# Two key copies trade engines, V7 moves by half a group, L0 passes a mask, and a memset moves two slots

## The chip, the cores and the metric

The kernel runs on one core of one Trainium2 chip. The metric is device time in microseconds. Before the change it was 331.88 us, the median of 3 runs (331.34 to 332.10). The profiled execution took 331.49 us, of which the profile spans 329.6 us, with TensorE granted its full clock throughout.

## The reference

Batched sparse attention is followed by a bilinear feed-forward network (FFN). Batch 8, 8 heads, 576 positions, 64 dimensions; half the heads see a local window of 32 positions, the other half see every 32nd position.

```python
scores = scale * np.matmul(q, k.transpose(0, 1, 3, 2))
mask_local = (rel >= 0) & (rel < stride)
mask_strided = (rel >= 0) & (pos[None, :] % stride == pos[:, None] % stride)
...
attn = attn / (np.sum(attn, axis=-1, keepdims=True) + 1e-09)
attn_out = np.matmul(attn, v)
...
x = attn_out.transpose(0, 2, 1, 3).reshape(B * S, H * D)     # 4608 x 512
out = (x @ w_a) * (x @ w_b) @ w_out                          # 512 -> 1536 -> 512
```

## The kernel before

The FFN runs over nine tiles of 512 tokens (t = 0 to 8). Each tile is sixteen slots: twelve of `ffn_ab`, which each make one 128-wide block of x @ w_a and x @ w_b on TensorE, copy the first product to SBUF on ScalarE (a_sb, L592) and multiply it with the second on VectorE (pf, L597), and four slots of output matmuls (`ffn_y`, L762, for tiles 0 and 1; `ffn_ys`, a form with fewer products, for tiles 2 to 8). Slot numbers run on, so slot 16 is the first of tile 1.

Attention is woven into these slots. The attention of batch 0 comes first, by the list `ORDER`. For each later batch a table places short steps at slot positions: `STEPS` for batches 1 and 2, `LATER` for the rest. A whole number means after that slot; a number ending in .5 means in the middle of the following slot (between the two FFN matmul groups, or after six of the twelve output matmuls). Batch 1 is spread over slots 5 to 15 of tile 0. The order of every engine is the order in which the program emits instructions; no scheduler changes it, so an instruction that waits holds up all that follow on its engine.

The steps have these names, where c is a pair of heads (0 and 1 local, 2 and 3 strided) and u is half of a pair (u = 2c or 2c + 1):

- Tk and Tq transpose keys and queries of pair c on TensorE into the PSUM tile tp, and copy them to SBUF in `T_e`: keys to kT1l (local) or kT1s (strided) at L306, queries at L314. For batch 1, line 306 puts the keys of c = 0 and c = 2 on ScalarE and those of c = 1 and c = 3 on VectorE.
- Pk and Pq (`pair_up`, L275) first bring two local heads side by side with a copy on VectorE, so that one transpose does both.
- S makes scores in the PSUM tile st (L383), exponentiates them on ScalarE into p (L391) and masks p with a bitwise AND on VectorE (L401).
- V multiplies p by the values into the PSUM tile o (L437), then takes a reciprocal (L445) and multiplies by it (L460), both on VectorE.
- X transposes the attention output into xT, which the FFN of tile 1 reads.
- L (`lead_vl`, L230) copies the leading 32 rows of each block of local values from the end of the block ahead of it, on VectorE. The second and later matmuls of V0 read what L0 writes.
- W (`fast_w`, L174) sums pairs of output weights on VectorE, for the tiles 2 to 8.

From slot 2 on there is one buffer of tp, one of o and one of st, and three buffers of mm for the FFN products. So the transposes of one step wait until the copy of the step ahead of it has emptied tp, and a V step waits until the multiply of the V step ahead of it has read o.

The table `at` places other work after a slot. `zero_qz` (L121) clears query buffers of two batches with memsets on VectorE; the four entries of buffer 0 (read from batch 2 on) come after slots 0, 2, 3 and 5. `spread_vs` (L246), also on VectorE, follows slots 6 to 9.

Of the kernel before, what the change touches and what calls it, by code (L numbers as in the profile page):

```python
# [16 lines left out]
RS = 8  # L17
NP = 72
GP = 80
# [3 lines left out]
PAD = 32  # L23
# [7 lines left out]
def kernel(  # L31
# [10 lines left out]
    nc = tc.nc  # L42
# [135 lines left out]
    def blocks(nm, z):  # L178
        z = int(z)
        return sb.tile([128, 2, (S, RS * GP)[z]], BF16, tag=f"t{nm}{z}", name=f"t{nm}{z}", bufs=1)  # L180
# [117 lines left out]
    def T_e(b, c, nm):  # L298
        tv = held.pop((b, c, nm))
        if c < 2:  # L300
            perm = lambda t: t.rearrange("d (p r) -> d p r", r=RL)
        else:
            perm = lambda t: t.rearrange("d (g p) -> d g p", p=GP)[:, :, :NP]
        if nm == "k":
            t = kT_buf[b % 2][c // 2][:, c % 2]
            (nc.scalar.copy if (b, c) in ((1, 0), (1, 2)) else nc.vector.tensor_copy)(perm(t[:, PAD:] if c < 2 else t[:, :RS * GP]), tv)  # L306
        elif b == 0:
            if c % 2 == 0:
                tl[b, c // 2, nm] = blocks("q", c // 2)
            nc.scalar.copy(perm(tl[b, c // 2, nm][:, c % 2]), tv)  # L310
        else:
            for j in range(2):
                pr = slice(64 * j, 64 * j + 64)
                (nc.vector.tensor_copy if (c, j) == (3, 1) else nc.scalar.copy)(  # L314
                    perm(qz_buf[b % 2][j][c // 2][pr, c % 2]), tv[pr])
# [38 lines left out]
    def step_Tk(b, c):  # L354
        T_p(b, c, "k")
        T_e(b, c, "k")

    def step_Tq(b, c):
        T_p(b, c, "q")
        T_e(b, c, "q")  # L360
# [159 lines left out]
    def step_X(b, c):  # L520
        X_p(b, c)
        X_e(b, c)

    PART = {"Tkp": lambda c: T_p(0, c, "k"), "Tke": lambda c: T_e(0, c, "k"), "Tqp": lambda c: T_p(0, c, "q"),
            "Tqe": lambda c: T_e(0, c, "q"), "Sp": lambda u: S_p(0, u), "Sx": lambda u: S_x(0, u),
            "Sm": lambda u: S_m(0, u), "Vp": lambda u: V_p(0, u), "Vr": lambda u: V_r(0, u), "Vn": lambda u: V_n(0, u),
# [7 lines left out]


    STEPS = {1: {5.5: "Tk2", 6: "Tk3", 6.5: "Tq2", 7.5: "S4 Tq3", 8: "S5", 8.5: "V4", 9: "S6 Pk0", 9.5: "V5 Pq0",
                 10: "Tk0 S7", 10.5: "V6 Tq0 Pk1", 11: "V7 Pq1", 11.5: "Tk1 S0 W0 W1", 12: "Tq1 W2", 12.5: "S1 X2 L0",
                 12.75: "V0 S2 W3", 13: "L1 V1 X3 W4", 13.5: "S3 X0", 14: "V2", 14.5: "V3", 15: "X1"},
             2: {20: "S0", 20.5: "S1", 21.5: "V0", 22: "S2", 23: "V1", 23.5: "S3", 24.5: "V2", 25: "S4", 26: "V3", 26.5: "S5",
                 27.5: "V4", 28: "S6", 28.5: "V5", 29: "S7", 29.5: "V6", 30.5: "V7"}}  # L540
# [246 lines left out]
    with tc.manual_schedule(engines={ENG.PE, ENG.SP, ENG.Pool, ENG.DVE, ENG.Activation}):  # L787
# [29 lines left out]
        for nm in ORDER:  # L817
            if nm[0] == "*":
                spin(int(nm[1:]))
            elif nm == "C0":  # L820
                for x, cp, n in ((raw[0], nc.vector.tensor_copy, "k"), (raw[1], nc.scalar.copy, "q")):
                    t = nats[0, n, False][:, 0:2].rearrange("p h r d -> p (h r d)")
# [42 lines left out]
        def do(i, fn, *args):  # L865
            at.setdefault(i, []).append(lambda: fn(*args))
# [29 lines left out]
            do(6 + h, spread_vs, 1, h, nc.vector.tensor_copy)  # L896
        do(1, zero_qz, 1, nc.vector, ((1, 1),))
        do(4, zero_qz, 1, nc.vector, ((1, 0),))
        for i, jz in ((2, (0, 0)), (3, (1, 0)), (0, (0, 1)), (5, (1, 1))):
            do(i, zero_qz, 0, nc.vector, (jz,))  # L900
        do(14, rezero, 1)
        do(27, fill_v, vl_buf[1])
# [53 lines left out]
```

## Time and profile before

| stretch, us | length | TensorE busy | VectorE busy | ScalarE busy | GpSimd busy |
|---|---|---|---|---|---|
| 28 to 36 | 8.00 | 7.81 | 3.94 | 3.72 | 7.74 |
| 36 to 44 | 8.00 | 7.89 | 7.83 | 5.72 | 3.40 |
| 44 to 52 | 8.00 | 6.48 | 5.90 | 4.36 | 4.15 |
| 52 to 62 | 10.00 | 9.89 | 7.51 | 5.42 | 6.84 |

Each row is a stretch of the span in which steps of batch 1 run; a busy time is the sum of the instructions' recorded time in it. A TensorE that is busy for nearly the whole stretch may still wait a little, because records overlap and a few are missing. What counts for the end is where TensorE stands still, and which engine's instruction it stands still for. The second row shows VectorE with hardly any free time, the first shows it half idle.

The change touches these instructions, with the times at which they start in the profiled execution:

| instruction | engine | start, us | duration, ns |
|---|---|---|---|
| memset qz01s (L121) | VectorE | 30.94 | 592 |
| key copy of Tk2, kT1s (L306) | ScalarE | 31.22 | 638 |
| V7's matmuls (L437) | TensorE | 44.46 | 8 matmuls, 0.42 us in all |
| key copy of Tk1, kT1l (L306) | VectorE | 47.04 | 746 |
| L0's copy, vl (L230) | VectorE | 51.02 | 422 |

### The profile page before, as it was taken

The numbers are of one execution on the slowest core, as the hardware profiler recorded it, in microseconds if no ns is written. First come the engines' busy times: TensorE is split into PE (matmuls) and PEld (weight loads), VectorE is DVE, ScalarE is ACT, GpSimd is POOL, SyncE is SP. The second block draws the span as 40 slices with busy tenths as digits, with TensorE's granted clock in tenths as the row PEclk, the third lists the DMA queues.
The fourth block names the chain that finished last, engine by engine and source line by source line (L and its number), as shares of the span: only waits on it lengthen the run. The fifth ranks groups of instructions, "written<-read, shape, count | busy, mean of one in ns | idle before, by whom it ended". The sixth has DMA issues, their size and how long they took to land.

```text
span 329.6 us, 7647 instructions
## 1 busy us (share of the span) xinstructions
PE 321.1 (97%) x2793; PEld 206.3 (63%) x2824; DVE 265.6 (81%) x509; ACT 201.1 (61%) x325; POOL 176.3 (53%) x294
## 2 busy tenths in 40 slices
PE   8999988999999999999999999999999999999995
PEld 6764555455555577556999995559555954584474
DVE  6757796889867999999999999999878944657662
ACT  5763756358778766887577756776787543313321
POOL 8946636897867655775577556855302131232021
PEclk9999999999999999999999999999999999999999
DMA  9999999599999699899998988998024022004004
GB/s 152 155 203 195 204 183 172 144 164 147 112 213 115 110 80 86 85 172 158 90 76 140 198 84 72 138 211 90 20 58 132 2 67 64 0 2 127 0 3 127
DMA packets 98837, 37.50 MB, mean 114 GB/s; under 512 B 76656, under 2 KB 95984, under 8 KB 98800
## 3 DMA queue, kind: packets, MB, share of 16 engines
q0 software_dynamic: 85936, 19.48, 66.0%
q1 hardware_dynamic: 12576, 17.34, 18.3%
q8 instruction: 22, 0.36, 0.5%
q10 hardware_dynamic: 288, 0.20, 0.2%
q14 instruction: 15, 0.12, 0.2%
HBM read 39.51 MB, written 9.44 MB: 149 GB/s over the span
## 4 chain that ended last, share of the span: by engine, by line
PE 83%; DMA 11%; POOL 4%; issue 1%; DVE 0%; POOLq 0%; ACT 0%; DVEq 0%
PE mm L575 50%; PE mm L680 17%; PE mm L762 5%; DMA wb_sb<-in_moe_w_b_dram 4%; DMA vl<-in_v_dram 4%; PE st L383 4%; PE o L481 4%; DMA shared<-in_q_dram 2%; PE mm L708 2%; DMA ql<-in_q_dram 1%; POOL wa_sb L251 1%; POOL wo_sb L254 1%; PE end L708 1%; POOL vs L109 1%; POOL wb_sb L251 0%
## 5 line engine op out<-in xcount | busy, mean ns | idle before, releaser
L575 PE MATMUL mm<-xT,wa_sb 128*128 128x512 bf16 (+1 forms) x453 | 108.9, 357 | 0.9
L575 PE MATMUL mm<-xT,wb_sb 128*128 128x512 bf16 (+1 forms) x466 | 109.4, 357 | 0.3
L592 ACT COPY a_sb<-mm 128x512 f32<-128x512 f32 x106 | 62.0, 585 | 47.6 <-PE mm L575 46.5
L922 POOL CAST pace<-pf 1x1 f32<-1x1 bf16 x84 | 31.3, 373 | 83.0 <-DVE pf L595 80.7
L575 PEld LDWEIGHTS <-wb_sb 128*128 128x128 bf16 x480 | 46.2, 98 | 43.9
L595 DVE TENSOR_TENSOR pf<-a_sb,mm 128x512 bf16<-128x512 f32 x84 | 56.4, 671 | 17.0 <-PE mm L575 13.8
L575 PEld LDWEIGHTS <-wa_sb 128*128 128x128 bf16 x480 | 42.7, 98 | 31.8 <-issue 0.2
L391 ACT ACTIVATE p<-st 128x576 bf16<-128x576 f32 (+1 forms) x64 | 41.5, 649 | 14.1 <-PE st L383 13.4
L490 ACT ACTIVATE xr<-o 64x576 f32<-64x576 f32 x48 | 31.1, 647 | 25.1 <-PE o L481 24.8
L680 PEld LDWEIGHTS <-ps 128*128 128x128 bf16 x360 | 34.5, 98 | 3.9
L491 ACT ACTIVATE xr<-xr 64x576 f32<-64x576 f32 x48 | 32.8, 683 | 1.5
L495 DVE TENSOR_TENSOR xT<-o,xr 64x288 bf16<-64x288 f32 x48 | 21.5, 447 | 7.6 <-ACT xr L491 7.1
L497 DVE TENSOR_TENSOR xT<-o,xr 64x288 bf16<-64x288 f32 x48 | 21.5, 448 | 6.4 <-ACT xr L491 5.3
L680 PE MATMUL mm<-wf,ps 128*128 128x256 bf16 x216 | 26.4, 273 | 0.0
L401 DVE TENSOR_TENSOR p<-p,mask_l 128x576 int16<-128x576 int16 x32 | 22.3, 696 | 2.4 <-ACT p L391 2.4
L762 PE MATMUL mm<-wo_sb,pf 128*128 128x512 bf16 x91 | 22.8, 379 | 0.2
L242 POOL DMA_DIRECT2D vs<-in_v_dram x24 | 19.6, 818 | 3.4 <-PE st L383 2.2
L211 POOL DMA_DIRECT2D kl<-in_k_dram x24 | 16.3, 678 | 7.4 <-issue 3.9
L597 DVE TENSOR_TENSOR pf<-a_sb,mm 128x512 bf16<-128x512 f32 x22 | 14.8, 672 | 5.8 <-ACT a_sb L592 4.9
L922 POOL COPY pace<-y_sb 1x1 f32<-1x1 f32 x16 | 2.8, 175 | 30.5 <-ACT y_sb L663 14.6
L211 POOL DMA_DIRECT2D ql<-in_q_dram x24 | 16.0, 666 | 5.2 <-DMA wo_sb<-in_moe_w_out_dram 4.1
L680 PE MATMUL mm<-wf,pf 128*128 128x256 bf16 x144 | 17.6, 273 | 0.0
(162 smaller groups left out, 503.1 us busy)
## 6 DMA issues: line engine op xcount, KB each, us to landing
out_dram<-y_sb SPq DMA_DIRECT2D x12, 512.0 KB, 4.8
out_dram<-y_sb SPq DMA_DIRECT2D x10, 256.0 KB, 3.2
vl<-in_v_dram POOLq DMA_DIRECT2D x6, 384.0 KB, 6.8
kl<-in_k_dram POOLq DMA_DIRECT2D x24, 72.0 KB, 3.1
ql<-in_q_dram POOLq DMA_DIRECT2D x24, 72.0 KB, 3.2
vs<-in_v_dram POOLq DMA_DIRECT2D x24, 72.0 KB, 3.7
wo_sb<-in_moe_w_out_dram POOLq DMA_DIRECT2D x4, 384.0 KB, 11.5
natk<-in_k_dram POOLq DMA_DIRECT2D x20, 72.0 KB, 3.5
```

Of the source, the lines that this page charges most:

```text
L211: nc.gpsimd.dma_start(out=t[32 * h:32 * h + 32], in_=src[b, h].rearrange("(i y) d -> y i d", y=32))
L391: nc.scalar.activation(p[:M, :, :W], st[:M, :, :W], ACT.Exp, scale=scale)
L401: nc.vector.tensor_tensor(pi, pi, mk, op=ALU.bitwise_and)
L490: nc.scalar.activation(r, sums, ACT.Ln)
L491: nc.scalar.activation(r, r, ACT.Exp, scale=-1.0)
L495: nc.vector.tensor_mul(dst[:, W * half:W * (half + 1)], o[:64, j, :W], r[:, j])
L575: nc.tensor.matmul(ps_[:, c0:c0 + n], lhsT=w[:, kk, 128 * f:128 * (f + 1)], rhs=xT[:, kk, x0:x0 + n], start=(kk == first and c0 == 0), sto ...
L592: nc.scalar.copy(a_sb, ab[0])
L595: nc.vector.tensor_mul(pf[:, f, :].rearrange("p (i a s) -> p a i s", i=2, s=16), halves(a_sb), halves(ab[1]))
L680: nc.tensor.matmul(bank[b][:, q], lhsT=lhs(g, q), rhs=rhs(g), start=new and q == 0 and g == 0, stop=g == FG - 1, skip_group_check=True)
L762: nc.tensor.matmul(ybank[j], lhsT=pf[:, f, 128 * j:128 * (j + 1)], rhs=wo_sb[:, f], start=(f == 0), stop=(f == FD - 1))
L922: nc.gpsimd.tensor_copy(pace, done)
```

## The change

Four edits of order and engine; nothing computed changes. The keys of batch 1 that go to ScalarE are now those of both local pairs (c = 0, 1) and not those of c = 0 and 2: Tk2's copy goes to VectorE and Tk1's to ScalarE. This is meant to leave ScalarE free for the FFN copies around slot 6 and VectorE free around slot 12. V7 moves from the end of slot 11 to the middle of slot 12, behind S0, so that TensorE need not wait there for the output tile o. L0 goes ahead of S1, so that VectorE does its copy before the mask of S1, which waits for ScalarE. And the memset of the strided half of query buffer (0, 1) moves from slot 5 to slot 7, which clears the place for Tk2's copy.

```diff
@@ T_e @@
-            (nc.scalar.copy if (b, c) in ((1, 0), (1, 2)) else nc.vector.tensor_copy)(perm(t[:, PAD:] if c < 2 else t[:, :RS * GP]), tv)
+            (nc.scalar.copy if b == 1 and c < 2 else nc.vector.tensor_copy)(perm(t[:, PAD:] if c < 2 else t[:, :RS * GP]), tv)
@@ STEPS @@
-                 10: "Tk0 S7", 10.5: "V6 Tq0 Pk1", 11: "V7 Pq1", 11.5: "Tk1 S0 W0 W1", 12: "Tq1 W2", 12.5: "S1 X2 L0",
+                 10: "Tk0 S7", 10.5: "V6 Tq0 Pk1", 11: "Pq1", 11.5: "Tk1 S0 V7 W0 W1", 12: "Tq1 W2", 12.5: "L0 S1 X2",
@@ zero_qz @@
-        for i, jz in ((2, (0, 0)), (3, (1, 0)), (0, (0, 1)), (5, (1, 1))):
+        for i, jz in ((2, (0, 0)), (3, (1, 0)), (0, (0, 1)), (7, (1, 1))):
             do(i, zero_qz, 0, nc.vector, (jz,))
```

## The prediction, made before the changed kernel was run

> **What bounds the kernel now.** I read the shares first, then TensorE's waits, then the timelines of the four engines around each wait.
>
> ```profile
> PE 321.1 (97%) x2793; PEld 206.3 (63%) x2824; DVE 265.6 (81%) x509; ACT 201.1 (61%) x325; POOL 176.3 (53%) x294
> ```
>
> TensorE (PE) has work nearly all the time, so only what moves its queue can move the end. Asked who TensorE waited for, the trace names three waits in the stretch that the diff touches (columns: total us, times, longest) and none from 62 us to the end:
>
> ```profile
> PE o L437 <- DVE vl L230: 0.7, 1, 0.7
> PE tp L286 <- DVE kT1l L306: 0.5, 1, 0.5
> PE o L437 <- DVE xr L460: 0.2, 1, 0.2
> ```
>
> Busy time by stretch agrees: TensorE has its holes between 44 and 52 us (6.48 of 8 us).
>
> ```profile
> 36.00:44.00 8.00, 7.89 (x91) 1.00 1.30 202
> 44.00:52.00 8.00, 6.48 (x72) 1.00 1.98 161
> ```
>
> The timeline (start, duration) shows the last hole's cause: VectorE (DVE) held the copy of leading rows behind a mask, and the mask behind ScalarE's exp.
>
> ```profile
> 49.84 0.65 ACT L391 ACTIVATE p<-st 128x576 bf16<-128x576 f32 x1 [0.28 <-PE st L383]
> ...
> 50.53 0.46 DVE L401 TENSOR_TENSOR p<-p,mask_l 128x576 int16<-128x576 int16 x1 [0.97 <-ACT p L391]
> ...
> 51.02 0.42 DVE L230 COPY vl<-vl 32x704 bf16<-32x704 bf16 x1
> 51.49 0.31 PE L437 MATMUL o<-vl,p 128*128 128x65 bf16 x5 [0.75 <-DVE vl L230]
> ```
>
> Two more holes are put down to nobody. The sixth FFN matmul group starts at 32.40, when ScalarE's copy ends (32.35), and the transposes of Tq2 start at 33.49, when VectorE's key copy ends (33.43):
>
> ```profile
> 31.22 0.64 ACT L306 COPY kT1s<-tp 128x576 bf16<-128x576 bf16 x1 [1.40 <-PE tp L295]
> 31.76 0.59 ACT L592 COPY a_sb<-mm 128x512 f32<-128x512 f32 x1
> ...
> 32.38 0.69 DVE L597 TENSOR_TENSOR pf<-a_sb,mm 128x512 bf16<-128x512 f32 x1 [0.85 <-ACT a_sb L592]
> ...
> 32.98 0.45 DVE L306 COPY kT1s<-tp 128x576 bf16<-128x576 bf16 x1
> ...
> 33.49 0.42 PE L295 MATMUL tp<-ident,shared 72*128 72x72 bf16 x8
> ```
>
> All holes together are some 1.9 us (0.2 + 0.2 + 0.22 + 0.50 + 0.75): a ceiling for the gain.
>
> [...] the trace has 638 ns for both ScalarE key copies, 451 ns for the strided keys and 746 ns for the local keys on VectorE. [...] the copy vs (L246) takes 279 ns alone and 451 ns at 40.90, beside a GpSimd DMA issue (40.53 to 41.26). I use that 0.17 us as what one collision costs.
>
> **The change, part by part.** Every operation and shape occurs in the trace of before, so only the waits are new.
>
> 1. *Tk2's key copy from ScalarE to VectorE.* ScalarE loses 638 ns at 31.22; VectorE gains 451 ns there, in the place of the memset (592 ns, 30.94) that leaves; it is otherwise idle to 32.38. The FFN copy a_sb can start when its matmuls end (30.9) and no longer holds the next group, so the hole at 32.40 goes. The product pf then waits for the other matmul group, ending at 32.05; one group earlier that wait ended 0.11 after the matmuls, so it starts at 32.16, not 32.38. The next key copy ends at 33.21 and Tq2 starts at 33.27: TensorE is **0.22 us ahead**.
>
> 2. *The memset of qz01s, 592 ns, two slots later.* It lands behind the copy vs at 36.48, in front of the mask of S4. From 35.88 to 44.67 VectorE shows no idle time at all: everything queued behind it (masks, normalisations, pair copies, pf) moves. Consecutive VectorE instructions overlap by 0.08, so it adds 0.51; part 1 brings the head of this queue 0.22 forward, so VectorE is 0.29 late. TensorE's weight load for V5 waits for the normalisation of V4, which ended at 39.75 and now at 40.04: load at 40.09, against 40.01. Tk0's load waits for the pair copy that ended at 40.98, now 41.27: load at 41.31, against 41.12. TensorE is now **0.19 us late**, having lost 0.41. V6 and Tq0 have 0.3 us of slack (42.19 to 42.49, 42.60 to 42.93) and wait no longer than that.
>
> 3. *V7 half a group later.* TensorE would be free at 44.24 + 0.19 = 44.43. It no longer waits for xr (0.22 gone) but does six output matmuls first (1.30). Tk1 starts at 45.73, against 46.01; S0 and V7 follow, and V7's work (0.25) is put back there. On VectorE V7's reciprocal and multiply (0.20 + 0.69) now stand behind the mask of S0.
>
> 4. *Tk1's key copy from VectorE to ScalarE.* ScalarE has ended a_sb by 45.5. The copy runs from 46.19 to 46.83 (638 ns), so Tq1, which TensorE reaches at about 47.15, does not wait: the 0.50 hole goes. The exp of S0 now queues behind it: 46.85 to 47.50, 0.12 later than before.
>
> 5. *L0 ahead of S1's mask.* L0's own input, the load of vl, has landed at 47.24. VectorE now does: mask of S0 47.55 to 48.00, V7 to 48.80, three wf (1.48 together) to 50.28, L0 50.20 to 50.62. V0's second matmul goes at 50.67 instead of 51.49. TensorE reaches V0 near 49.9, so it still waits some 0.75 there: the wait stays, but on a chain that starts earlier. The mask of S1 moves behind L0, to 51.0; V1 needs it at 52.2. It is free.
>
> Sum at V0: **0.82 us ahead**. Behind it every step hangs on TensorE's progress (reciprocals after V0, then S2, X3, L1), and after 62 us TensorE waited for nobody, so I carry the lead to the end: 331.88 - 0.82 = 331.06, rounded to 331.1.
>
> **The rivals.**
>
> A, *the memset is absorbed*: VectorE regains its 0.29 before V5 and Tk0, TensorE keeps its 0.22 and the whole chain to V0 moves 0.41 more: 331.06 - 0.41 = 330.65. [...] Against: no idle in 35.88 to 44.67.
>
> B, *the memset passes in full*: the head of the VectorE queue does not move (0.51 late, plus one collision of 0.17, so 0.68). Tk0's load is at 41.7, TensorE is 0.58 late instead of 0.19, and V0 goes at 51.06: 331.06 + 0.39 = 331.45. For it: TensorE hangs on VectorE at 40.0 and 41.1 with 0.1 us to spare. Against: GpSimd's issues are few there.
>
> C, *the new chain to V0 becomes the bound*, so it is slower: mask, reciprocal, multiply, three wf and L0 now stand in line from S0's exp. If each of these seven is hit by a collision (7 x 0.17 = 1.2) on top of B's 0.39, V0 goes at 52.26, 0.77 later than before: 331.88 + 0.77 = 332.65. For it: GpSimd issues DMAs at 47.52, 49.52 and from 50.17. Against: wf kept 546 ns beside those issues before.
>
> A fourth possibility gives no change: the lead is lost later, where VectorE is 97% busy (110 to 130 us), leaving 331.9. TensorE shows no wait on VectorE there, and VectorE's work moves along with it.
>
> **How the numbers follow.** Forecast 0.50, A 0.13, B or the later loss 0.25, C 0.12. The bar of 0.2% is 0.66 us, and the forecast clears it by 0.16 only, so of its 0.50 I count 0.42 as faster and 0.08 as same. B and the later loss give same 0.22 and slower 0.03. Faster 0.55, same 0.30, slower 0.15. The range goes from a little under A, 330.4, to the later loss with some scatter of the runs (331.34 to 332.10), 332.0; C is left out.
>
> **What would show it.** Step 1: Tq2's transposes start near 33.3. Step 2: the memset lies near 36.5, and Tk0's transposes start later than 41.33, near 41.5. Step 3: no wait for xr near 44.2. Step 4: no wait of tp for kT1l. Step 5: a wait of V0 for vl of 0.6 to 0.9 us ending near 50.7. The prediction is wrong if Tk1 starts later than 46.0, if V0's wait ends after 51.2, or if TensorE shows waits after 62 us that before did not have.

## The result, and the profile after

The changed kernel took 330.38 us (median of 6 runs, 329.97 to 330.96), against 331.61 us for the kernel before in the same series: a ratio of 0.9964, 95% interval 0.9949 to 0.9979. Measured once more on another occasion it gave 330.74 us against 331.58 us, ratio 0.9976 (0.9966 to 0.9987). So the change saves 0.8 to 1.2 us, and both intervals lie below 1. The forecast was 0.8.

TensorE's waits over the whole span of the changed kernel (total us, times, longest us); the first stands at the kernel's start and was there before too:

```profile
PE misc L153 <- PEq L940: 0.9, 1, 0.9
PE mm L762 <- DMA wo_sb<-in_moe_w_out_dram: 0.7, 1, 0.7
```

All three waits of before are gone, V0's wait for L0 too, and one has come that the prediction did not name: output matmuls (L762) wait for a load of wo_sb, the output weights. TensorE's busy time in the two stretches shown before (length, busy, granted clock, DMA share, GB/s):

```profile
36.00:44.00 8.00, 7.95 (x88) 1.00 1.32 202
44.00:52.00 8.00, 7.34 (x87) 1.00 1.81 151
```

The stretch with the holes went from 6.48 to 7.34 us busy. What remains is mostly the new wait, seen in the timeline (start, duration) of four engines:

```profile
45.46 0.64 ACT L306 COPY kT1l<-tp 128x576 bf16<-128x576 bf16 x1 [0.53 <-PE tp L286]
...
45.99 0.66 ACT L391 ACTIVATE p<-st 128x576 bf16<-128x576 f32 x1
46.58 0.81 PE L762 MATMUL mm<-wo_sb,pf 128*128 128x512 bf16 x3 [0.66 <-DMA wo_sb<-in_moe_w_out_dram]
...
47.90 1.48 DVE L174 TENSOR_TENSOR wf<-wo_sb 128x768 bf16<-128x768 bf16 x3
...
49.41 0.35 DVE L230 COPY vl<-vl 32x704 bf16<-32x704 bf16 x1
...
49.94 0.34 PE L437 MATMUL o<-vl,p 128*128 128x65 bf16 x6
```

The key copy and the exp lie one behind the other on ScalarE, as step 4 has it. TensorE then stands still for the third of the four pieces of wo_sb. VectorE does not stand still meanwhile: it runs through its line to L0, which ends at 49.76, and V0's six matmuls go in one piece at 49.94.

**How the runs are compared.** The profiled spans differ by 1.5 us (329.6 and 328.1), but not all of that is the change: Tk2's first transpose, ahead of which TensorE has the same instructions in every kernel, starts at 30.76 and 30.26 us, and over all profiles here between 30.23 and 31.15. From the first FFN matmul of tile 1 to the end it is 269.4 to 269.5 us in every profile in which that matmul is recorded. So I read each profile from Tk2's first transpose to tile 1's first matmul: 29.35 us before, 28.33 after. Where that last record is missing I take V3's first matmul plus 1.89 us, the distance in all the others. The stretch falls into five parts, by the first matmul of each step:

| kernel | Tk2 to Tq2 | Tq2 to Tk0 | Tk0 to Tk1 | Tk1 to Tq1 | Tq1 to tile 1 | sum | ratio to before, 95% interval |
|---|---|---|---|---|---|---|---|
| before | 2.73 | 7.84 | 4.68 | 1.83 | 12.27 | 29.35 | |
| changed | 2.52 | 8.17 | 4.05 | 2.22 | 11.37 | 28.33 | 0.9964 (0.9949 to 0.9979) |
| after_again | 2.52 | 8.30 | 4.05 | 1.41 | 12.04 | 28.32 | 0.9976 (0.9966 to 0.9987) |
| l0_alone | 2.74 | 7.84 | 4.57 | 1.94 | 11.37 | 28.46 | 0.9978 (0.9971 to 0.9985) |
| v7_alone | 2.74 | 7.83 | 4.04 | 1.64 | 12.20 | 28.45 | 0.9972 (0.9961 to 0.9983) |
| keys_alone | 2.52 | 8.17 | 4.66 | 1.62 | 12.20 | 29.17 | 0.9987 (0.9979 to 0.9995) |
| memset6 | 2.51 | 7.84 | 4.04 | 1.41 | 12.02 | 27.82 | 0.9944 (0.9930 to 0.9958) |
| memset5 | 2.51 | 7.84 | 4.04 | 1.41 | 12.02 | 27.82 | 0.9958 (0.9944 to 0.9971) |
| no_l0 | 2.51 | 8.16 | 4.05 | 1.41 | 12.39 | 28.52 | 0.9979 (0.9970 to 0.9988) |
| no_v7 | 2.52 | 8.41 | 4.65 | 1.21 | 11.39 | 28.18 | 0.9959 (0.9947 to 0.9971) |
| no_keys | 2.74 | 7.83 | 4.05 | 1.63 | 11.61 | 27.86 | 0.9964 (0.9952 to 0.9976) |
| no_wo_wait | 2.51 | 8.33 | 4.05 | 1.41 | 12.18 | 28.48 | 0.9974 (0.9967 to 0.9981) |
| w_late | 2.51 | 7.84 | 4.04 | 2.37 | 11.37 | 28.13 | 0.9938 (0.9924 to 0.9952) |
| best | 2.51 | 7.84 | 4.04 | 1.41 | 11.37 | 27.17 | 0.9939 (0.9927 to 0.9951) |

Most parts repeat to 0.01 or 0.02 us where the same wait ends them, so one profile tells more of an edit than the times do, whose intervals are 0.5 to 1.0 us wide. The part from Tq2 to Tk0 is an exception where the memset stands in it: 8.16 to 8.41.

### The profile page after: what moved, and what is told of

It reads as the page before. It is cut to its first block, busy times and chain, and to the rows that moved or that the text cites. A ratio compares the mean times of both kernels' runs of the same rounds, so it can differ in the third digit from the quotient of the medians.

```text
span 328.1 us, 7680 instructions
## 1 busy us (share of the span) xinstructions
PE 322.6 (98%) x2824; PEld 206.5 (63%) x2824; DVE 265.7 (81%) x509; ACT 201.2 (61%) x325; POOL 176.7 (54%) x294
## 4 chain that ended last, share of the span: by engine, by line
PE 84%; DMA 9%; POOL 5%; issue 1%; POOLq 0%; ACT 0%; DVE 0%; DVEq 0%
PE mm L575 51%; PE mm L680 17%; PE mm L762 6%; DMA shared<-in_q_dram 5%; PE st L383 4%; DMA wo_sb<-in_moe_w_out_dram 4%; PE o L481 4%; POOL shared L196 2%; PE mm L708 2%; POOL wa_sb L251 1%; POOL vl L224 1%; PE end L708 1%; POOL wb_sb L251 0%; POOL tk L237 0%; PE tp L506 0%
## 5 line engine op out<-in xcount | busy, mean ns | idle before, releaser
L575 PE MATMUL mm<-xT,wa_sb 128*128 128x512 bf16 (+1 forms) x472 | 110.3, 357 | 0.0
L762 PE MATMUL mm<-wo_sb,pf 128*128 128x512 bf16 x96 | 23.4, 379 | 0.7 <-DMA wo_sb<-in_moe_w_out_dram 0.7
```

The costliest lines, as they stand in the source:

```text
L575: nc.tensor.matmul(ps_[:, c0:c0 + n], lhsT=w[:, kk, 128 * f:128 * (f + 1)], rhs=xT[:, kk, x0:x0 + n], start=(kk == first and c0 == 0), sto ...
L762: nc.tensor.matmul(ybank[j], lhsT=pf[:, f, 128 * j:128 * (j + 1)], rhs=wo_sb[:, f], start=(f == 0), stop=(f == FD - 1))
```

## The experiments

### Each edit alone

**L0 ahead of S1, alone (l0_alone).**

```diff
-12.5: "S1 X2 L0"
+12.5: "L0 S1 X2"
```

> The kernel before with the leading-row copy L0 ahead of S1 as the only edit. 'The stretch' is the time from the first FFN matmul of slot 6 to the first FFN matmul of tile 1: 30.22 us in the profile of before (29.89 to 60.11), 29.38 in that of after (29.21 to 58.59). Theory, each edit's gain depends on which wait ends last: VectorE is free after the three weight sums (49.55 before), L0 runs there to 49.9, and V0, which TensorE reaches at 50.55, doesn't wait: the stretch is 0.75 shorter, 29.5, the time 0.7 us lower. Rival, the load of vl sets L0: L0 is no earlier than before and nothing changes.

The part from Tq1 to tile 1 went from 12.27 to 11.37, and V0 no longer waits; the ratio of 0.9978 is 0.7 us. L0 was free to start at 49.4 and the load of vl did not hold it. The theory stands. (I read from Tk2, not from slot 6's first matmul, because Tk2's transposes waited 0.3 for a load here.)

**V7 half a group later, alone (v7_alone).**

```diff
-11: "V7 Pq1", 11.5: "Tk1 S0 W0 W1"
+11: "Pq1", 11.5: "Tk1 S0 V7 W0 W1"
```

> The kernel before with V7 in the middle of slot 12 as the only edit. Theory: TensorE starts the output matmuls 0.38 earlier (44.08), Tk1's key copy on VectorE no longer stands behind V7's normalisation and ends near 47.0, so Tq1 starts some 0.8 earlier, and S1, its mask and L0 follow: V0's wait stays but ends near 50.6: the stretch is some 0.9 shorter, 29.3. Rival, V7's normalisation now stands in the chain to L0 and takes the gain back: the stretch is 0.0 to 0.3 shorter.

Tk0 to Tk1 fell by 0.64 (0.25 of it V7's own matmuls, which come after Tk1 now) and Tk1 to Tq1 by 0.19 although V7 is now within it. The sum is 0.90 shorter, the time 0.93 us (331.41 x 0.0028). V0's wait stays, as the theory has it:

```profile
PE o L437 <- DVE vl L230: 0.7, 1, 0.7
```

**The keys and the memset, alone (keys_alone).**

```diff
-nc.scalar.copy if (b, c) in ((1, 0), (1, 2)) else nc.vector.tensor_copy
+nc.scalar.copy if b == 1 and c < 2 else nc.vector.tensor_copy
-(0, (0, 1)), (5, (1, 1))
+(0, (0, 1)), (7, (1, 1))
```

> The kernel before with the two key copies exchanged and the memset after slot 7, V7 and L0 where they were. Theory: the memset costs V5, Tk0 and V7 0.3 together, the exchange takes the 0.50 wait of Tq1 away; V0's wait for L0 stays and ends some 0.4 earlier: stretch 29.8. Rival, the memset is free (VectorE's queue has slack): 0.7 shorter, 29.5.

The exchange brings Tq2 0.21 forward, the memset holds Tk0 0.33 back, and the part with Tq1 is 0.21 shorter although a load stood in it here (TensorE's waits):

```profile
PE o L437 <- DVE vl L230: 0.7, 1, 0.7
PE mm L762 <- DMA wo_sb<-in_moe_w_out_dram: 0.3, 1, 0.3
PE o L437 <- DVE xr L460: 0.2, 1, 0.2
```

The sum is 0.18 shorter, not the theory's 0.4; the load's 0.3 would account for the difference. In the times it is 0.4 us (0.9987). The memset is not free, so the rival falls. The three edits alone bring 0.89 + 0.90 + 0.18 = 1.97 us, and together 1.02: they work on the same holes.

### One edit taken back

**L0 back (no_l0).**

```diff
-12.5: "L0 S1 X2"
+12.5: "S1 X2 L0"
```

> The changed kernel with L0 behind S1 and X2 again. Theory, waits stand in series and the last one counts: L0 goes behind S1's mask (49.91 to 50.37 in the profile of after), V0's second matmul starts near 50.7 instead of 49.98, and the time from Tk2's first transpose to the first FFN matmul of tile 1 (29.35 us before, 28.33 after) is some 0.7 longer, 29.0; time 0.6 to 0.7 above the changed kernel's. Rival, VectorE's chain to L0 is late anyway: within 0.2 of after.

This missed: 28.52 is 0.2 longer than with all four edits, not 0.7, which is what the rival had. VectorE's timeline tells why:

```profile
48.02 1.48 DVE L174 TENSOR_TENSOR wf<-wo_sb 128x768 bf16<-128x768 bf16 x3
49.42 0.45 DVE L401 TENSOR_TENSOR p<-p,mask_l 128x576 int16<-128x576 int16 x1
49.90 0.35 DVE L230 COPY vl<-vl 32x704 bf16<-32x704 bf16 x1
```

In the kernel before, VectorE stood idle for 0.97 ahead of that mask, waiting for the exp. With V7 moved, its line is longer and the exp has come (48.54 + 0.65 = 49.19) before VectorE gets to the mask. L0 then loses only the 0.45 of the mask itself: the last part is 12.39 against 12.04 in after_again, 0.35 longer. The sum is only 0.2 longer because the part with the memset happens to be 0.14 shorter here. So with the other edits in, L0's own edit is worth 0.2 to 0.35, not 0.9.

**V7 back (no_v7).**

```diff
-11: "Pq1", 11.5: "Tk1 S0 V7 W0 W1"
+11: "V7 Pq1", 11.5: "Tk1 S0 W0 W1"
```

> The changed kernel with V7 back at the end of slot 11. Alone this edit took 0.9 us. Theory, the edits cover each other: V7's wait for o comes back (0.3), but the output matmuls behind it waited 0.66 for the third piece of wo_sb in the profile of after, so this wait shrinks by as much, and VectorE's chain to L0 has V7's 0.9 less to do after S0: 0 to 0.3 above the changed kernel. Rival, gains add: 0.9 above it.

Nothing is lost: 28.18, 0.15 less than with all four edits, and a ratio of 0.9959. Its wait for xr is back, but there is neither the wait for wo_sb nor that for L0:

```profile
44.27 0.42 PE L437 MATMUL o<-vs,p 72*128 72x65 bf16 x8 [0.19 <-DVE xr L460]
...
49.76 0.36 PE L437 MATMUL o<-vl,p 128*128 128x65 bf16 x6
```

So the edit that brings 0.9 alone brings nothing as the last of the four. The sum lies a little below what the theory allowed (0 to 0.3 above the changed kernel); its point, that the edits cover each other, stands, and the rival (gains add) falls.

**Keys and memset back (no_keys).**

```diff
-nc.scalar.copy if b == 1 and c < 2 else nc.vector.tensor_copy
+nc.scalar.copy if (b, c) in ((1, 0), (1, 2)) else nc.vector.tensor_copy
-(0, (0, 1)), (7, (1, 1))
+(0, (0, 1)), (5, (1, 1))
```

> The changed kernel with the key copies and the memset as before; V7 and L0 moved. Theory, the exchange and the memset together bring less than they cost once the other two edits are in: V5 and Tk0 no longer wait for VectorE (0.33), Tk1's key copy (746 ns on VectorE) ends before TensorE needs tp, and L0 starts near 50.0 as with V7 alone, where V0's second matmul stood at 50.97 and now comes at 50.35: from Tk2 to tile 1 27.8, 0.5 shorter than after. Rival, the exchange is worth its 0.5 wait at Tq1: 28.8, 0.4 longer than after.

27.86, as the theory gave (27.8): 0.47 shorter than the changed kernel. The ratio, 0.9964, is the same as the changed kernel's first one, so the times don't show this half microsecond, and the changed kernel's second ratio (0.9976) doesn't exclude it. In the parts, without the memset Tk0 comes 0.34 to 0.47 earlier after Tq2; without the exchange Tq2 comes 0.22 later. The rest differs with the wait that stood there: TensorE does not wait for wo_sb, as in the first profile (1.63 against 2.22), and not as long for L0 as in after_again (11.61 against 12.04).

### The memset, and the new wait

**The memset after slot 6, or back after slot 5 (memset6, memset5).**

```diff
-(0, (0, 1)), (7, (1, 1))
+(0, (0, 1)), (6, (1, 1))      # memset6;  (5, (1, 1)) in memset5
```

> The changed kernel with the memset of qz01s after slot 6 instead of 7, where VectorE is idle in the profile of after (33.85 to 35.17). Both theories: V5 and Tk0 no longer wait, TensorE is 0.33 earlier at S7. Theory, a DMA floor: the output matmuls after V7 wait for the third piece of wo_sb as before (0.66 us in the profile of after), the wait grows by the same 0.33, and the time is that of the changed kernel within 0.1 where the load is late. Rival, TensorE's queue alone counts: the stretch is 0.33 shorter than after's 29.38, 29.05.

> The changed kernel with the memset of qz01s after slot 5, where before had it: ahead of Tk2's key copy, which is on VectorE now. Theory: the memset (592 ns, from about 0.1 before Tk2's transposes) delays that copy by some 0.3, Tk3's transposes and the next FFN copies take no harm from it (0 to 0.1), and V5 and Tk0 no longer wait: from Tk2 to tile 1 27.9, as with slot 6, so that moving the memset to slot 7 is a loss of 0.3 within the change. Rival, the move was needed for the key copy: Tq2's transposes come 0.2 or more later after Tk2 than the 2.51 of the changed kernel.

Both give 7.84 from Tq2 to Tk0, as before, and 27.82 in all, 0.5 less than with the memset after slot 7; Tq2 comes 2.51 after Tk2 in both, so the place after slot 5 did not have to be cleared. memset5 differs from no_keys (27.86) by the exchange of the key copies alone: as the last edit in, with the memset left in its place, the exchange is worth 0.04. With slot 6 the memset lies in idle time (VectorE):

```profile
33.54 0.59 DVE L121 MEMSET qz01s<- 128x640 uint32 x1
```

The load of wo_sb was early in these two profiles, so they say nothing on the theory that it is a floor. By time, slot 6 gives 0.9944; its interval lies below that of after_again and overlaps the changed kernel's first one.

**The wait for wo_sb taken away (no_wo_wait).**

```diff
-rhs=wo_sb[:, f]
+rhs=wo_sb[:, f % 6 if t == 0 and j == 0 and f < 9 else f]
```

> The changed kernel in which the seventh to ninth output matmuls of the first 128 tokens read pieces 0 and 1 of wo_sb in the place of piece 2, so that they don't wait for its load (the first 128 rows of the output are computed with other weights). Theory, the wait for wo_sb (0.66 in the profile of after) only hides a wait for L0: V0's second matmul can't start before L0 ends (49.76), it started at 49.98, so at most 0.2 is gained. Rival, the load is the bound: 0.66 gained.

(The three matmuls read piece 0; a piece is three of the twelve blocks f.) Nothing is gained: 28.48, and a ratio of 0.9974 over 22 runs, where the rival's 0.66 us would give 0.9944 to 0.9956. The profile by itself is no test, because in it the load was early: GpSimd's wait for the piece ended at 46.08, and TensorE came to these matmuls at 46.51. It shows the same wait for L0 as after_again (the second line is Tk2's own wait, ahead of the stretch):

```profile
PE o L437 <- DVE vl L230: 0.7, 1, 0.7
PE tp L295 <- DMA shared<-in_k_dram: 0.5, 1, 0.5
```

**The changed kernel again (after_again).**

> The changed kernel once more, for a second profile of it. Theory: the wait for the third piece of wo_sb changes from run to run with the loads; where it is short, V0 waits for L0 instead (0.5 to 0.9), and Tk2 to tile 1 stays between 28.2 and 28.6. Rival: the wait is always 0.6 to 0.7 and V0 never waits.

The sum is the same to 0.01, but the holes are others: no wait for wo_sb, and V0 waits for L0 until 50.72, the wait that step 5 of the prediction described. The first line below is Tk2's own wait, ahead of the stretch; the third is Tk0's, behind the memset.

```profile
PE tp L295 <- DMA shared<-in_k_dram: 0.7, 1, 0.7
PE o L437 <- DVE vl L230: 0.5, 1, 0.5
PE tp L286 <- DVE tq L275: 0.3, 1, 0.3
```

Whether TensorE stands for the load (up to 46.58 in the first profile) or for L0 (up to 50.72 in this one) depends on how late the load is against TensorE in that run. In the first profile the wait for the load (0.66) covered the later one for L0. That the two sums agree to 0.01 is chance: in w_late, below, the same wait holds the stretch with L0 out of the way.

### A version that beats both

**Weight sums out of L0's line (w_late), and the output matmuls reordered as well (best).** Both have the memset after slot 6.

```diff
-11.5: "Tk1 S0 V7 W0 W1", 12: "Tq1 W2"
+11.5: "Tk1 S0 V7", 12: "Tq1"
+for n in range(3): do(28 + n, fast_w, n, slice(0, 3))
# best only: output matmuls of tile 0, groups y0 and y1, pieces of wo_sb by f
-y0 f0-5 | Tk1 S0 V7 | y0 f6-8 | Tq1 | y1 f0-5          | L0 S1 X2 | y1 f6-8
+y0 f0-5 | Tk1 S0 V7 | y1 f0-2 | Tq1 | y1 f3-5, y0 f6-8 | L0 S1 X2 | y1 f6-8
```

The last two lines are a sketch of the order, not code: f counts the twelve 128-row blocks of the weights, three to a piece of wo_sb, and a bar stands where steps of batch 1 come in.

> The changed kernel with the memset after slot 6 and the first three weight sums (1.48 us of VectorE, read from tile 2 on) taken out of the line ahead of L0 and put after slots 28 to 30. Theory: with L0 near 48.1 V0 waits for nothing, and only the load of wo_sb can still hold TensorE: Tk2 to tile 1 27.2 where that load is early (the sum of the shortest pieces seen, 2.51 + 7.84 + 4.04 + 1.41 + 11.37), up to 27.8 where it is late; time 0.3 to 0.6 below that with the memset after slot 6. Rival, vl lands too late for L0: no better than 27.8.

> As w_late, and the output matmuls of the first 256 tokens in another order: three of the second group's (weights of piece 0) take the place of the three of the first group that read piece 2 of wo_sb, which come 1.1 us later. Theory: the load has landed by then in any run; 27.2 from Tk2 to tile 1 always, and a time 0.1 to 0.4 below w_late's. Rival: another wait (a free bank for the second group, the loads of vl) takes its place: as w_late.

In w_late V0 waits for nothing (11.37), but the load held TensorE longer than I allowed for:

```profile
46.59 0.81 PE L762 MATMUL mm<-wo_sb,pf 128*128 128x512 bf16 x2 [0.81 <-DMA wo_sb<-in_moe_w_out_dram]
```

28.13 is outside the 27.2 to 27.8 of the theory, and the time, 0.9938 against memset6's 0.9944, is not clear of it. In best all five parts are at their shortest at once, 27.17, and from Tk2 on TensorE waits for nobody. By time the two are alike, 0.9938 and 0.9939: either saves 2.0 us of 331.6, and the 0.1 to 0.4 us that best should have gained on w_late is not seen. Both intervals lie below that of after_again and overlap the changed kernel's first one by a little. That best's shorter stretch is not seen in its time fits the starts: its Tk2 started at 31.15, w_late's at 30.47, so V3 starts at 56.43 and 56.71, only 0.28 apart. An early TensorE would give back to the loads what it had; this is read from two profiles and was not tried by itself.

## Why the prediction was right, point by point

The forecast of 0.82 us is close to the lower of the two measured gains (1.2 and 0.8), and it is smaller than the 1.02 us that the trace shows in both profiles of the changed kernel. Some of the agreement is luck. The times alone can't tell the forecast (331.06) from rival A (330.65), since 330.38 and 330.74 were measured; 330.38 lies at the low edge of the range that was given, in part because the kernel before came out 0.3 lower in that series than the 331.88 it was reckoned from. And the first profile reached its 1.02 us by a wait that the prediction did not have. What bears it out is the trace, point by point. Times there are compared from Tk2's start, because Tk2 starts 0.50 earlier in the first profile than before, and 0.26 later in after_again.

1. *Tk2's copy on VectorE, 0.22.* Measured 0.21: from 2.73 to 2.52 in every kernel that has the exchange, and not in those that lack it.

2. *The memset, 0.41 late at Tk0.* Measured 0.33 in one profile and 0.46 in the other. It lies behind the copy vs and ahead of the mask of S4 as forecast, and V5 (0.21 and 0.24 of it) and Tk0 wait behind it:

```profile
36.14 0.59 DVE L121 MEMSET qz01s<- 128x640 uint32 x1
```

The 0.13 between the profiles goes with a collision like that of the copy vs in the prediction: in after_again the pair copy for Tk0 took 0.45 us beside a GpSimd DMA issue (40.96 to 41.63), where it took 0.35 in the first profile. The six profiles with the memset after slot 7 agree: 8.16 or 8.17 where that copy took 0.35, and 8.30, 8.33 and 8.41 where it took 0.45 to 0.49.

```profile
41.33 0.45 DVE L275 COPY tq<-shared 96x768 bf16<-96x768 bf16 x1
```

Rival A, the memset absorbed, is refuted by memset6 (7.84 there); of rival B the collision came in three of the six, and not the rest.

3. *V7, 0.22 for the wait.* This is the term that was mis-sized. Tk0 to Tk1 fell by 0.63, of which 0.25 is V7's work put behind Tk1: the wait had cost 0.38. The record's idle time is shorter than the loss, because each matmul record reaches some 0.16 into the next one when nothing waits (before, the transposes at 42.95 are recorded to 43.37, and the next group starts at 43.21); the 44.24 at which the prediction has TensorE free is such a recorded end. It is the same for the other holes: Tq1's was recorded as 0.50 and cost 0.67 (1.83 against 1.41 less V7's 0.25), V0's as 0.75 and cost 0.90 (12.27 against 11.37). With 0.22 for Tq2, 0.38, 0.67 and 0.90 make 2.17 us. That is what best took out (29.35 - 27.17 = 2.18). The ceiling of 1.9 in the prediction was too low.

4. *Tk1's copy on ScalarE.* No wait of tp for kT1l is left. Tk1 to Tq1 is 1.41 where no load stands in it, as forecast (1.42). The exp of S0, though, starts 0.53 after the start of the key copy ahead of it (45.46 and 45.99 in the first profile), not the 0.66 of the prediction: it had allowed for the overlap of consecutive instructions on VectorE (0.08), and not on ScalarE, where the record of the key copy reaches 0.11 into that of the exp (45.46 + 0.64 = 46.10).

5. *V0's wait stays, on an earlier chain.* The wait is there in after_again, memset6, memset5 and no_wo_wait, and not in the first profile, where the wait for wo_sb stood in its place. In after_again it was 0.51 (forecast 0.6 to 0.9) and ended 19.70 after Tk2's start. The forecast's 50.67 is 19.91 after it, so V0 went 0.21 earlier than forecast, though the two clock times (50.72 and 50.67) look alike. V7's mis-sized wait, less what the memset cost more, is 0.10 of this, and ScalarE's overlap 0.13; the rest cancels.

The prediction looked at the landing of vl, L0's input, but not at that of wo_sb's third piece. Before, TensorE came to the matmuls that read it 0.64 us after GpSimd's wait for the piece had ended:

```profile
45.88 0.66 POOL L211 DMA_DIRECT2D ql<-in_q_dram  x1 [1.54 <-DMA wo_sb<-in_moe_w_out_dram]
46.52 0.81 PE L762 MATMUL mm<-wo_sb,pf 128*128 128x512 bf16 x3
```

Where TensorE itself waits for the piece, GpSimd's wait ends 0.24 or 0.25 after TensorE's (46.82 and 46.58 in the first profile; keys_alone and w_late agree), so the margin before was some 0.9 us. In the first profile TensorE would have come 0.76 earlier (at 45.76), which alone would not have used it up; the piece also landed 0.94 later. In after_again (second line below) it landed 0.64 earlier than in the first profile (first line), and there was no wait:

```profile
46.82 0.66 POOL L211 DMA_DIRECT2D ql<-in_q_dram  x1 [2.04 <-DMA wo_sb<-in_moe_w_out_dram]
46.18 0.66 POOL L211 DMA_DIRECT2D ql<-in_q_dram  x1 [1.41 <-DMA wo_sb<-in_moe_w_out_dram]
```

Why the load was late in three of the profiles is not shown.

6. *The lead carries to the end.* Right: 269.5 us from tile 1 to the end before and after, so the lead was not lost later. Rival C fell: V0 went earlier, not later, and the three weight sums took 1.48 us together in the changed kernel too. One instruction of that chain, L0, did meet a collision in no_wo_wait (0.51 us long, where it takes 0.35 alone).

## What to carry to other kernels

Gains of edits that work on waits in series don't add: here edits worth 0.9, 0.9 and 0.2 us alone made 1.0 together. As the last one in, by the stretch, L0's edit was worth 0.2 us, V7's lost 0.15, and the keys with the memset lost 0.5, all of it the memset's new place. So try each edit of a set by taking it back, too. Before moving work earlier, list for each instruction that comes earlier how long ago its loads had landed; here a margin of some 0.9 us was used up by 0.8 us of lead and a load that came 0.9 us later. And a place on a second engine was free here only where that engine's timeline shows idle time: the memset cost nothing after slots 5 and 6 and 0.3 to 0.6 us after slot 7, on an engine busy for half of one stretch and nearly all of the next (3.94 and 7.83 of 8 us before).

## What the runs showed of the hardware

A recorded wait of TensorE understates the loss by about 0.16 us in this kernel (0.22, 0.50 and 0.75 recorded, 0.38, 0.67 and 0.90 lost; 0.66 and 0.81 for the wait for wo_sb in the first profile). This is a matter of the record, in which a matmul reaches some 0.16 into the next one (before, 43.37 against 43.21, as in point 3).

The load times vary enough between executions of the same code to change which wait is seen: GpSimd's wait for the third piece of wo_sb ended at 46.82 in one profile of the changed kernel and at 46.18 in the other.

What a collision of a VectorE copy (L230 and L275, 0.35 us alone) with a GpSimd DMA issue cost here depended on where in the issue the copy began. Over all fourteen profiles, in the thirteen cases in which such a copy was slowed, it began 0.24 to 0.44 us into the issue and ended 0.15 to 0.16 us after the issue's end, up to 0.58 us long (before, the copy at 42.10 began 0.31 into an issue of 0.66 us and took 0.50). A copy that began earlier, up to about 0.25 us into the issue, kept its 0.35 us, and then the issue was the longer one: before, the copy at 40.63 began 0.10 into an issue of 0.73 us, and in no_l0 the one at 42.14 began 0.25 into an issue of 0.88 us, where 0.66 is usual. So now the copy and now the issue was the longer one, and the prediction's 0.17 us is not a fixed price.
